# An attention and mixer kernel on one core: tables, first normalizations and transform pieces of the front dealt out over its steps

## The chip, the core and the metric

The kernel runs on one core of a Trainium2 chip. A core has a matrix engine (TensorE, PE in the profile; its weight loads are a row of their own, PEld), a vector engine (DVE), a scalar engine (ACT), a general engine (POOL) and a queue of transfers (SP). Each engine takes its instructions in the order in which they are written for it, and waits at an instruction until what it reads is there and the place it writes is free. Products are accumulated in PSUM, and from there DVE and ACT fetch them; the other tiles lie in SBUF. The metric is the device time of one execution, in microseconds (us): the kernel before took 987.98 in the median of three runs.

## The reference

Three stages follow one another. Inputs are 4 batches, 8 heads, 576 tokens, 64 numbers per head.

```python
# 1. attention in a window of 64 keys
scores = scale * q @ k.T                        # scale = 1/8
scores = where(0 <= query - key < 64, scores, -1e9)
x = softmax(scores) @ v                         # -> [4, 576, 512]
# 2. Fourier mixing, then a channel mixer
u = x + real(fft(fft(x, axis=1), axis=2))
un = (u - mean(u)) / sqrt(var(u) + 1e-6)        # per token
x = u + relu(un @ w_ch1) @ w_ch2                # 512 -> 2048 -> 512
# 3. token mixer, then a second channel mixer
h = relu(x.T @ w_tok1) @ w_tok2                 # 576 -> 256 -> 576
u = x + h.T
out = u + relu(u @ w_ch1b) @ w_ch2b             # 512 -> 1536 -> 512
```

The weights of the mixers come as 64-bit floats.

## The kernel before

**Precision.** Products of stages 2 and 3 are made of two parts of each number: `split` (L125) casts a tile to a rounded 32-bit format on ACT (L127, the `hi` part) and subtracts this from the source on DVE (L130, the `lo` part); three products (hi hi, hi lo, lo hi) stand for one.

**Stage 1** is cut into 36 units, nine for each batch: a tile of 128 queries and four of the eight heads. Unit k goes through scores `s` on PE (L353, L360), their maximum `mx` on DVE (`a_mx`, L369), the exponentials `pb` on ACT (L379), a transposition `pt` on PE (L386) with its copy on ACT (`a_cp`, L389), the product `o` with V on PE (L399), and a division on DVE.

**The transforms** of stage 2 are one per batch. `fold` (L425) adds and subtracts rows of `x` that lie mirrored, and splits the result (tiles `pmt`, `eo`, `xh`; the middle rows in `fold_m`, `xs`). `fft` (from L458) is a generator of 16 chunks: eight of the first transform along the tokens (`zp`, evicted and split as `zt`, L477), two of a small rest (`zx`), and six of the second one along the channels (`bp`, `ap`, tile `t3`), whose results POOL adds to `x`. They multiply by constant tables: `cs` (two tiles of 3 x 320 columns, `load_cs`) and `dd` (4 x 258 columns, `load_dd`), with a row `nyq`.

**The normalization** `prep` (L598) of a group of 384 rows takes their mean and variance on DVE, writes normalized rows `una` on ACT, transposes them on PE (`tpa`, L629) and splits them into `aT`.

**The weights** are converted by `converter` (L148): one piece of 128 x 512 goes through ACT (L162), five DVE instructions (L163 to L165, L178, L179), a multiplication by the exponent on POOL (L181; on DVE once `tailing` is over 10), a cast on ACT (L174) and a subtract on DVE (L184). A call of `conv(1)` takes one of the three parts of such a conversion.

**The channel mixer** runs over six groups of 384 rows and 16 pieces f of the hidden width. `gemm1` (L638) makes twelve matmuls into `zg`; `gemm1_ev` takes the positive part on ACT (L645) and its rest on DVE (L646, `hh`); `gemm2` (L656) makes nine into `acc`, three products later. The first two groups go together through the f, so 32 products use each weight as it is converted; the rest follows in a second pass.

**What sets the order.** All this is written in `front_body` (L863) inside a hand-made schedule: what the Python code calls first stands first in each engine's queue. A loop of 39 steps k issues the stages of units k, k-1 and k-2, up to two chunks of a transform, and then side work as long as a budget `left` lasts: each step adds `CFG["dve"]` = 3.35 less the unit's own work, each piece takes off an estimate. The first table is split at k = 3, the second at 5, `dd` at 7; conversions begin at k = 8; `prep` of group 0 begins at 20 and of group 1 at 30. Behind the loop the rest of the transform of the last batch is written in a tail of chunks n, with a step of the channel mixer (`next(gph)`) at every fourth n, a part of a conversion at odd n, and a part of group 1's `prep` at even ones. After that the mixer goes on alone, one `conv` after each product. DMAs of inputs are asked for in front of the loop and at fixed steps in it, on SP's queue.

## Time and profile before

| | |
|---|---|
| runs | 986.79, 987.98, 988.15 us (median 987.98) |
| the profiled execution | 986.48 us, of which 984.7 are the span of the trace |
| PE, busy | 948.2 us (96%) |
| PE weight loads | 817.7 us (83%) |
| DVE | 521.6 us (53%), 1067 instructions |
| ACT | 288.9 us (29%), 647 instructions |
| POOL | 104.1 us (11%) |
| DMA | 105.47 MB, mean 107 GB/s |

The span is the time from the first to the last instruction in the trace. The page shows these shares in 40 slices of 24.6 us each:

```profile
PE   8998988599999999999999999999999999999998
...
DVE  3777677899999265677675324456321212121121
ACT  4655554333333223232232212223211111111110
POOL 0003032242222001112111000000000000000000
PEclk9789989799999999999999999999999999999999
```

Each digit is a busy share in tenths; PEclk is the clock granted to PE in tenths of its full speed. The loop over the units ends in slice 7, the first two groups of the channel mixer run up to about slice 13. From there the DVE has little to do. A shown share of PE near 90% is not PE at its peak, since the ends of its matmuls are modelled.

### The profile page before, as it was taken

The page shows a single profiled execution, that of the slowest core. Times are in us where ns is not written, and L with a number is a line of the kernel's source. Part 1 is how long each engine was busy: PE and PEld are TensorE (multiplying, and loading weights), DVE is VectorE, ACT ScalarE, POOL GpSimd, SP SyncE. Part 2 cuts the span into 40 slices and gives each one's busy share as a digit, 9 for nine tenths or more (in the row PEclk, how much of TensorE's full clock was granted, in tenths as well). Part 3 has the DMA queues.
Part 4 walks back from the last instruction along what each step waited for, and adds up shares of the span by engine and source line. Part 5 has one row for each costly group of instructions (what it writes and reads, how often), then busy time and mean ns, then how long its engine had stood idle before and what let it go on. Part 6 is the DMA issues. An engine that isn't in the chain of part 4 may idle for free.

```text
span 984.7 us, 14125 instructions
## 1 busy us (share of the span) xinstructions
PE 948.2 (96%) x5576; PEld 817.7 (83%) x5576; DVE 521.6 (53%) x1067; ACT 288.9 (29%) x647; POOL 104.1 (11%) x108
## 2 busy tenths in 40 slices
PE   8998988599999999999999999999999999999998
PEld 5676766588887899999999988878999999999997
DVE  3777677899999265677675324456321212121121
ACT  4655554333333223232232212223211111111110
POOL 0003032242222001112111000000000000000000
PEclk9789989799999999999999999999999999999999
DMA  9843320234353052454543216377110100101010
GB/s 335 283 136 124 115 66 23 91 117 135 118 151 96 14 180 75 145 180 152 180 163 130 80 31 217 109 252 234 29 65 1 56 10 31 35 4 61 1 33 33
DMA packets 56454, 105.47 MB, mean 107 GB/s; under 512 B 5058, under 2 KB 25604, under 8 KB 56004
## 3 DMA queue, kind: packets, MB, share of 16 engines
q1 hardware_dynamic: 55700, 104.24, 32.6%
q8 instruction: 44, 0.72, 0.3%
q10 hardware_dynamic: 688, 0.33, 0.1%
q14 instruction: 22, 0.18, 0.1%
HBM read 79.78 MB, written 24.77 MB: 106 GB/s over the span
## 4 chain that ended last, share of the span: by engine, by line
PE 67%; DVE 13%; issue 1%; ACT 1%; DMA 1%; POOL 0%; DVEq 0%; SPq 0%; ACTq 0%; POOLq 0%
PE zg L638 31%; PE acc L656 31%; PE zt L753 2%; PE zt L728 2%; DVE we L165 2%; DVE wm L179 2%; PE tpa L629 1%; DVE w2s L184 1%; DVE w1s L184 1%; DVE hh L646 1%; DVE rw L178 1%; DVE we L163 1%; DVE we L164 1%; DMA x2r<-x_d 0%; DMA x_d<-o 0%
## 5 line engine op out<-in xcount | busy, mean ns | idle before, releaser
L638 PE MATMUL zg<-aT,w1s 128*128 128x384 f32 x2016 | 388.7, 340 | 3.9 <-DVE hh L646 2.9
L656 PE MATMUL acc<-w2s,hh 128*128 128x512 f32 x1512 | 381.5, 394 | 0.0
L638 PEld LDWEIGHTS zg<-aT,w1s 128*128 128x128 f32 x2016 | 354.9, 189 | 25.9 <-DVE hh L646 13.0
L656 PEld LDWEIGHTS acc<-w2s,hh 128*128 128x128 f32 x1512 | 281.4, 188 | 51.6
L646 DVE SCALAR_TENSOR_TENSOR hh<-zg,hh 128x384 fp32r<-128x384 f32 x168 | 93.3, 556 | 283.6 <-ACT hh L645 283.4
L645 ACT ACTIVATE hh<-zg 128x384 fp32r<-128x384 f32 x168 | 82.4, 491 | 380.5 <-PE zg L638 380.3
L181 POOL TENSOR_TENSOR wm<-wm,we 128x512 f32<-128x512 f32 (+2 forms) x64 | 70.6, 1104 | 346.9 <-DVE wm L179 300.7
L162 ACT ACTIVATE wm<-rw 128x512 f32<-128x512 uint32 (+2 forms) x66 | 41.9, 634 | 78.7 <-DVE w2s L184 40.3
L130 DVE TENSOR_TENSOR aT<-tpa,aT 128x512 fp32r<-128x512 f32 x36 | 24.9, 692 | 41.3 <-ACT aT L127 41.2
L179 DVE SCALAR_TENSOR_TENSOR wm<-rw,wm 128x512 f32<-128x512 int32 (+2 forms) x66 | 43.4, 658 | 5.2
L386 PE MATMUL pt<-ident,pb 128*128 128x128 f32 x144 | 34.0, 333 | 11.1 <-ACT pb L379 10.9
L165 DVE SCALAR_TENSOR_TENSOR we<-rw,we 128x512 uint16<-128x512 uint16 (+2 forms) x66 | 43.5, 659 | 2.0
L360 PE MATMUL s<-kT,qT 64*64 64x128 f32 x576 | 43.3, 294 | 0.0
L360 PEld LDWEIGHTS s<-kT,qT 64*64 64x64 f32 x576 | 34.0, 144 | 10.8 <-issue 10.8
L379 ACT ACTIVATE pb<-s,nb 128x128 f32<-128x128 f32 x144 | 41.2, 369 | 1.3
L386 PEld LDWEIGHTS pt<-ident,pb 128*128 128x128 f32 x144 | 19.1, 149 | 21.7 <-ACT pb L379 13.5
L127 ACT CAST aT<-tpa 128x512 fp32r<-128x512 f32 x36 | 21.0, 586 | 53.2 <-PE tpa L629 53.2
L399 PEld LDWEIGHTS o<-vt,pb 128*64 128x64 f32 x576 | 22.0, 151 | 10.2 <-ACT pb L389 4.5
L399 PE MATMUL o<-vt,pb 128*64 128x65 f32 x576 | 27.3, 243 | 3.2 <-ACT pb L389 3.2
L178 DVE TENSOR_SCALAR rw<-rw 128x512 int32<-128x512 int32 (+2 forms) x66 | 27.6, 418 | 2.0
L163 DVE TENSOR_SCALAR we<-rw 128x512 uint16<-128x512 uint16 (+2 forms) x66 | 28.3, 429 | 0.6 <-DMA rw<-in_moe_w_ch_dram 0.2
L369 DVE TENSOR_REDUCE mx<-s 128x4 f32<-128x512 f32 x36 | 24.5, 682 | 6.3 <-PE s L360 6.3
(128 smaller groups left out, 747.1 us busy)
## 6 DMA issues: line engine op xcount, KB each, us to landing
rw<-in_moe_w_ch_dram SPq DMA_DIRECT2D x56, 512.0 KB, 3.7
vt<-in_vx_dram SPq DMA_DIRECT2D x16, 520.0 KB, 6.7
ur<-u_d SPq DMA_DIRECT2D x28, 256.0 KB, 4.1
wb_d<-wm SPq DMA_DIRECT2D x24, 256.0 KB, 3.0
rf<-wb_d SPq DMA_DIRECT2D x12, 512.0 KB, 4.3
kT<-in_kt_dram SPq DMA_DIRECT2D x3, 1536.0 KB, 10.7
qT<-in_qt_dram SPq DMA_DIRECT2D x8, 512.0 KB, 5.2
x_d<-o SPq DMA_DIRECT2D x16, 256.0 KB, 3.4
```

Source lines behind the costliest of these rows:

```text
L162: held("a", nc.scalar.activation(out=m, in_=low, func=AF.Copy, scale=2.0 ** -52, bias=1.0))
L165: nc.vector.scalar_tensor_tensor(out=e, in0=top, scalar=0x8000, in1=e, op0=ALU.bitwise_and, op1=ALU.bitwise_or)
L179: nc.vector.scalar_tensor_tensor(out=m, in0=high, scalar=2.0 ** -20, in1=m, op0=ALU.mult, op1=ALU.add)
L181: eng.tensor_tensor(out=m, in0=m, in1=e.bitcast(BF16), op=ALU.mult)
L360: nc.tensor.matmul(s4[64 * bl:64 * bl + 64, c, :], lhsT=q_t[b, t // 2][64 * r:64 * r + 64, c, q0:q0 + 64], rhs=kT[b][64 * r:64 * r + 64, c ...
L379: nc.scalar.activation(out=pb[:, 0, c], in_=s4[:, c], func=AF.Exp, bias=nb[:, c:c + 1], scale=scale)
L386: nc.tensor.transpose(pt[:, c, :], pb[:, 0, c, :], ident)
L399: mm = nc.tensor.matmul(o[64 * bl:64 * bl + 64, c, :], lhsT=pb[:, 1, c, 64 * bl:64 * bl + 64], rhs=rhs)
L638: nc.tensor.matmul(zp, lhsT=W[f, 0][:, a, d, :], rhs=res["aT"][:, c, d, :], start=n == 0, stop=n == 11)
L645: nc.scalar.activation(out=h[:, 0], in_=zp, func=AF.Relu)
L646: nc.vector.scalar_tensor_tensor(out=h[:, 1], in0=zp, scalar=0.0, in1=h[:, 0].bitcast(F32), op0=ALU.max, op1=ALU.subtract)
L656: nc.tensor.matmul(res["acc"][c], lhsT=h[:, a, 128 * c:128 * c + 128], rhs=W[f, 1][:, w, :], start=f == 0 and i == 0, stop=f == NF - 1 and ...
```

## The change

It does five things, all in the front. (1) The tables are split in ten pieces, one a step from k = 1 on, and `nyq` in a piece of its own; before, whole at k = 3, 5 and 7. (2) Transform chunks of batch b begin at k = 9b + 13 at the earliest, and in the steps with k % 9 of 2 or 3 one is issued and not two; more of the last transforms comes to stand in the tail. (3) Conversions in the loop begin at k = 11 and not 8. (4) `prep` of group 0 begins at k = 21 and writes its three `una` before the first transposition; its last parts are given a step each from k = 28 on, and those of group 1 one or two a step from k = 31 (`q1`), ten of them inside the loop. (5) Behind the loop a mixer step stands at once, the folds that are left are finished, and the tail has fixed places: mixer steps at six n (`tg`), parts of `prep` at three (`tp`), parts of conversions at eleven (`tc`).

```diff
     def load_cs(g):
...
-        def go():
-            hi = blk([128, 3, KN], F32R, name="cs_hi")
-            lo = blk([128, 3, KN], F32R, name="cs_lo")
-            split(hi, lo, rt, nc.scalar, nc.vector)
-            for j in range(3):
-                csm[divmod(3 * g + j, 2)] = (hi[:, j, :], lo[:, j, :])
-        return go
+        hi = blk([128, 3, KN], F32R, name="cs_hi")
+        lo = blk([128, 3, KN], F32R, name="cs_lo")
+        for j in range(3):
+            csm[divmod(3 * g + j, 2)] = (hi[:, j, :], lo[:, j, :])
+        return [lambda j=j: split(hi[:, j], lo[:, j], rt[:, j], nc.scalar, nc.vector) for j in range(3)]
...
     def load_dd():
...
+        out = [lambda j=j: split(hi[:, j], lo[:, j], rt[:, j], nc.scalar, nc.vector) for j in range(4)]
+        out.append(lambda: nc.vector.tensor_copy(out=nyq, in_=r))
+        return out
...
     def prep(l, src, g, norm, res, keep=True, pt=pm, ts=None):
...
+        ahead = manual[0] and keep
+        if ahead:
+            us = []
+            for c in range(NCH):
+                us.append(unit(c))
+                yield 0.1
         for c in range(NCH):
...
+            a = us[c] if ahead else unit(c)
+            if not ahead:
+                yield 0.1
             tp = pt("tpa").rearrange("p (c n) -> p c n", c=4)
...
     def gphase(l, W, NF, src, dst, norm, extra):
...
-                else:
+                elif not tailing[0]:
                     next(nxt, None)
...
     def front_body():
...
-            later = [load_cs(0), load_cs(1)]
+            later = load_cs(0) + load_cs(1)
...
             def chunk():
                 while cur or ffts:
                     if not cur:
+                        if k < 9 * ffts[0] + 13:
+                            return None
                         cur.append(fft(ffts.pop(0)))
...
-                for _ in range(2):
-                    e = chunk() if k >= 2 else None
+                for _ in range(1 if k % 9 in (2, 3) else 2):
+                    e = chunk() if k >= 13 else None
...
+                if k >= 28 and side0:
+                    t = next(side0[0], None)
...
+                if k == 30:
+                    pre1[0] = prep(0, u_d, 1, True, res[1, 0], ts=x_of(1))
+                for _ in range(2 if k >= NU else 1):
+                    if k >= CFG["q1"] and qcount < 10:
+                        left -= next(pre1[0])
+                        qcount += 1
                 while side and left > 0.0:
...
-                if k in (3, 5):
+                if k >= 1 and later:
                     later.pop(0)()
-                    left -= 1.1
+                    left -= 0.4
                     if k == 3:
-                        later.append(load_dd())
-                if k == 7:
-                    later.pop(0)()
+                        later += load_dd()
...
-                if k == 20:
+                if k == 21:
                     side0.append(prep(0, u_d, 0, True, res[0, 0], ts=x_of(0)))
...
-                while k >= 8 and left > 0.0 and njob[0] < 2 * KA:
+                while k >= 11 and left > 0.0 and njob[0] < 2 * KA:
...
+            next(gph)
+            for t in side:
+                drain(t)
...
             n = 0
             tailing[0] = 1
             while True:
-                if n % 4 == 0:
+                if n in CFG["tg"]:
                     next(gph)
...
-                if n % 2:
+                if n in CFG["tp"]:
+                    next(pre1[0], None)
+                elif n in CFG["tc"]:
                     conv(1)
-                elif n >= 4:
-                    next(pre1[0], None)
...
+ 'q1': 31,
+ 'tg': (2, 4, 6, 9, 11, 14),
+ 'tp': (3, 5, 7),
+ 'tc': (4, 6, 8, 9, 10, 11, 12, 13, 14, 15, 16),
```

In the listings that follow, a row is one kind of instruction (line, operation, out<-in, shape) in the order of its engine. The lines of the changed kernel are 3 lower up to the change in `prep`, and 7 higher behind it.

ACT, at the first table `cs`. Before, from the copy `pb<-pt` of unit 0 on:

```order
L389 COPY pb<-pt 128x512
L371 ACTIVATE nb<-mx 128x4
L379 ACTIVATE pb<-s_178,nb 128x128 x4
L389 COPY pb<-pt 128x512
L371 ACTIVATE nb<-mx 128x4
L379 ACTIVATE pb<-s_205,nb 128x128 x4
L389 COPY pb<-pt 128x512
L371 ACTIVATE nb<-mx 128x4
L379 ACTIVATE pb<-s_245,nb 128x128 x4
L127 CAST cs_hi<-r_cs 128x960
L389 COPY pb<-pt 128x512
```


And now, from the same place:

```order
L386 COPY pb<-pt 128x512
L368 ACTIVATE nb<-mx 128x4
L376 ACTIVATE pb<-s_182,nb 128x128 x4
L127 CAST cs_hi<-r_cs 128x320
L386 COPY pb<-pt 128x512
L368 ACTIVATE nb<-mx 128x4
L376 ACTIVATE pb<-s_211,nb 128x128 x4
L127 CAST cs_hi<-r_cs 128x320
L386 COPY pb<-pt 128x512
```


The cast of the whole table stood behind the exponentials of unit 3. Its first third now stands behind those of unit 1 and ahead of unit 1's copy, and the second third one step later.

DVE, between two neighbouring rows `hh` of the first two groups in the tail. Before:

```order
L646 SCALAR_TENSOR_TENSOR hh<-zg,hh 128x384
L527 TENSOR_TENSOR t_2596<-ap,t_2596 64x257
L528 TENSOR_TENSOR t_2596<-ap,t_2596 64x257
L184 TENSOR_TENSOR w1s<-wm,w1s 128x512
L163 TENSOR_SCALAR we<-rw 128x512
L164 TENSOR_SCALAR we<-we 128x512
L165 SCALAR_TENSOR_TENSOR we<-rw,we 128x512
L178 TENSOR_SCALAR rw<-rw 128x512
L179 SCALAR_TENSOR_TENSOR wm<-rw,wm 128x512
L646 SCALAR_TENSOR_TENSOR hh<-zg,hh 128x384
```


And now, between the rows that answer to them (the end of the stretch is shown):

```order
L163 TENSOR_SCALAR we<-rw 128x512
L164 TENSOR_SCALAR we<-we 128x512
L165 SCALAR_TENSOR_TENSOR we<-rw,we 128x512
L178 TENSOR_SCALAR rw<-rw 128x512
L179 SCALAR_TENSOR_TENSOR wm<-rw,wm 128x512
L184 TENSOR_TENSOR w2s<-wm,w2s 128x512
L163 TENSOR_SCALAR we<-rw 128x512
L164 TENSOR_SCALAR we<-we 128x512
L165 SCALAR_TENSOR_TENSOR we<-rw,we 128x512
L178 TENSOR_SCALAR rw<-rw 128x512
L179 SCALAR_TENSOR_TENSOR wm<-rw,wm 128x512
L653 SCALAR_TENSOR_TENSOR hh<-zg,hh 128x384
```


Before, one conversion (L163 to L179) and one subtract (L184) stand between two hh. Now two conversions stand there.

PE, at the first product of the channel mixer (`zg`), after the loop. Before:

```order
L523 MATMUL ap<-nyq,zx 64x258 x2
L477 MATMUL zp<-cs_hi,xh 128x320
L477 MATMUL zp<-cs_lo,xh 128x320
L477 MATMUL zp<-cs_hi,xh 128x320 x2
L477 MATMUL zp<-cs_lo,xh 128x320
L477 MATMUL zp<-cs_hi,xh 128x320
L477 MATMUL zp<-cs_hi,xs 128x320
L477 MATMUL zp<-cs_lo,xs 128x320
L629 MATMUL tpa<-ident,una 128x128 x4
L638 MATMUL zg<-aT,w1s 128x384 x12
```


And now:

```order
L645 MATMUL zg<-aT,w1s 128x384 x12
L636 MATMUL tpa<-ident,una 128x128 x4
L517 MATMUL ap<-dd_hi,zt 64x258
L517 MATMUL ap<-dd_lo,zt 64x258
L517 MATMUL ap<-dd_hi,zt 64x258 x2
L517 MATMUL ap<-dd_lo,zt 64x258
L517 MATMUL ap<-dd_hi,zt 64x258
L520 MATMUL ap<-nyq,zx 64x258 x2
L474 MATMUL zp<-cs_hi,xh 128x320
L474 MATMUL zp<-cs_lo,xh 128x320
L474 MATMUL zp<-cs_hi,xh 128x320 x2
L645 MATMUL zg<-aT,w1s 128x384 x12
```


Before, a whole chunk pair `zp` of the last transform and the transposition `tpa` stand ahead of the first `zg`. Now `zg` stands first, and `tpa`, the last part of batch 2's transform (`ap`) and half a `zp` stand between it and the second one.

## Rows read from the trace of the kernel before

**Rows 1.** Windows: from:to, length, busy of PE, PEld, DVE, ACT, POOL, clock, DMA share, GB/s.
```profile
25.00:35.00 10.00, 10.00 (x85) 7.76 (x86) 7.05 (x17) 6.35 (x19) 0.00 (x0) 0.50 0.75 251
162.40:235.00 72.60, 58.25 (x324) 49.42 (x324) 63.63 (x124) 27.07 (x55) 25.50 (x27) 0.88 0.33 106
235.00:319.70 84.70, 82.63 (x393) 68.94 (x392) 80.46 (x149) 30.05 (x57) 22.09 (x19) 1.00 0.41 121
```

**Rows 2.** DVE timeline, units: start, us, line, op, tiles, shapes, count, [idle before, releaser].
```profile
14.21 0.69 DVE L369 TENSOR_REDUCE mx<-s 128x4 f32<-128x512 f32 x1 [1.73 <-PE s L360]
...
21.40 1.16 DVE L130 TENSOR_TENSOR cs_lo<-r_cs,cs_hi 128x960 fp32r<-128x960 f32 x1 [3.30 <-ACT cs_hi L127]
22.47 0.68 DVE L369 TENSOR_REDUCE mx<-s 128x4 f32<-128x512 f32 x1
...
23.81 0.68 DVE L369 TENSOR_REDUCE mx<-s 128x4 f32<-128x512 f32 x1
...
36.50 1.23 DVE L130 TENSOR_TENSOR dd_lo<-r_dd,dd_hi 128x1032 fp32r<-128x1032 f32 x1 [2.65 <-ACT dd_hi L127]
...
55.74 0.68 DVE L369 TENSOR_REDUCE mx<-s 128x4 f32<-128x512 f32 x1
```

**Rows 3.** ACT timeline around the first table.
```profile
13.68 1.15 ACT L379 ACTIVATE pb<-s,nb 128x128 f32<-128x128 f32 x4
...
20.37 0.99 ACT L127 CAST cs_hi<-r_cs 128x960 fp32r<-128x960 f32 x1 [0.67 <-DMA r_cs<-in_c_cs_dram]
...
23.43 1.14 ACT L379 ACTIVATE pb<-s,nb 128x128 f32<-128x128 f32 x4
```

**Rows 4.** PE timeline, the first matmul of the scores of two neighbouring units.
```profile
28.97 0.63 PE L353 MATMUL s<-cap,idb 128*128 128x512 bf16 x1
...
33.41 0.63 PE L353 MATMUL s<-cap,idb 128*128 128x512 bf16 x1
```

**Rows 5.** Groups by shape, 10 to 205 us: busy us, mean ns, idle before, releaser.
```profile
L425 DVE TENSOR_TENSOR pmt<-xp 128x512 f32<-128x512 f32 x5 | 4.7, 941 | 0.0
...
L130 DVE TENSOR_TENSOR zt<-zp,zt 128x320 fp32r<-128x320 f32 x16 | 7.9, 492 | 15.1 <-ACT zt L127 15.1
...
L127 ACT CAST zt<-zp 128x320 fp32r<-128x320 f32 x16 | 7.0, 437 | 1.7 <-PE zp L477 1.7
...
L425 DVE TENSOR_TENSOR pmt<-x 128x512 f32<-128x512 f32 x3 | 2.1, 688 | 0.1
```

**Rows 6.** DVE timeline from the last unit's maximum to the eighth hh.
```profile
162.40 0.66 DVE L369 TENSOR_REDUCE mx<-s 128x4 f32<-128x512 f32 x1
...
186.86 0.56 DVE L646 SCALAR_TENSOR_TENSOR hh<-zg,hh 128x384 fp32r<-128x384 f32 x1 [0.23 <-ACT hh L645]
...
216.05 0.55 DVE L646 SCALAR_TENSOR_TENSOR hh<-zg,hh 128x384 fp32r<-128x384 f32 x1
...
230.57 0.55 DVE L646 SCALAR_TENSOR_TENSOR hh<-zg,hh 128x384 fp32r<-128x384 f32 x1
231.03 1.40 DVE L184 TENSOR_TENSOR w2s<-wm,w2s 128x512 fp32r<-128x512 f32 x1
232.36 0.41 DVE L163 TENSOR_SCALAR we<-rw 128x512 uint16<-128x512 uint16 x1
...
235.00 0.55 DVE L646 SCALAR_TENSOR_TENSOR hh<-zg,hh 128x384 fp32r<-128x384 f32 x1
```

**Rows 7.** PE timeline after the last unit.
```profile
174.74 0.63 PE L477 MATMUL zp<-cs_hi,xh 128*128 128x320 f32 x1 [4.48 <-ACT xh L127]
...
182.24 4.06 PE L638 MATMUL zg<-aT,w1s 128*128 128x384 f32 x12 [0.68 <-ACT aT L127]
...
188.48 2.28 PE L638 MATMUL zg<-aT,w1s 128*128 128x384 f32 x12
```

**Rows 8.** DVE timeline behind the last conversion of the first two groups.
```profile
324.81 0.56 DVE L646 SCALAR_TENSOR_TENSOR hh<-zg,hh 128x384 fp32r<-128x384 f32 x1 [3.69 <-ACT hh L645]
...
328.94 0.56 DVE L646 SCALAR_TENSOR_TENSOR hh<-zg,hh 128x384 fp32r<-128x384 f32 x1 [3.58 <-ACT hh L645]
```

More of the change, by code (lines that the diff above doesn't have):

```diff
@@ L287, in load_dd @@
             ldq.dma_start(out=rt[:, 2 * m:2 * m + 2, :], in_=c_dd[m])
-        def go():
-            nc.vector.tensor_copy(out=nyq, in_=r)
-            hi = blk([128, 4, LN], F32R, name="dd_hi")
-            lo = blk([128, 4, LN], F32R, name="dd_lo")
-            split(hi, lo, rt, nc.scalar, nc.vector)
-            for m in range(2):
-                for cs in range(2):
-                    ddm[m, cs] = (hi[:, 2 * m + cs, :], lo[:, 2 * m + cs, :])
-        return go
+        hi = blk([128, 4, LN], F32R, name="dd_hi")
+        lo = blk([128, 4, LN], F32R, name="dd_lo")
+        for m in range(2):
+            for cs in range(2):
+                ddm[m, cs] = (hi[:, 2 * m + cs, :], lo[:, 2 * m + cs, :])
+        out = [lambda j=j: split(hi[:, j], lo[:, j], rt[:, j], nc.scalar, nc.vector) for j in range(4)]
+        out.append(lambda: nc.vector.tensor_copy(out=nyq, in_=r))
+        return out
     kT = {}
@@ L618, in prep, with unit @@
         res["aT"] = aT
-        for c in range(NCH):
-            u = ts[c]
-            if norm:
-                a = un([128, DM], F32, name="una")
-                nc.scalar.activation(out=a, in_=u, func=AF.Identity, scale=y[:, c:c + 1], bias=nm[:, c:c + 1])
-            else:
-                a = u
-            yield 0.1
+        def unit(c):
+            if not norm:
+                return ts[c]
+            a = un([128, DM], F32, name="una")
+            nc.scalar.activation(out=a, in_=ts[c], func=AF.Identity, scale=y[:, c:c + 1], bias=nm[:, c:c + 1])
+            return a
+        ahead = manual[0] and keep
[4 more added lines that the diff above has]
+                yield 0.1
+        for c in range(NCH):
+            a = us[c] if ahead else unit(c)
+            if not ahead:
+                yield 0.1
             tp = pt("tpa").rearrange("p (c n) -> p c n", c=4)
@@ L825, in gphase @@
                             ncount[0] += 1
-                else:
+                elif not tailing[0]:
                     next(nxt, None)
@@ L919, in front_body @@
                         side.append(fold_m(b))
+                if k >= 28 and side0:
+                    t = next(side0[0], None)
+                    if t is None:
+                        side0.pop(0)
+                    else:
+                        left -= t
+                if k == 30:
[4 more added lines that the diff above has]
+                        qcount += 1
                 while side and left > 0.0:
@@ L954, in front_body @@
                         load_q(b, 2)
-                if k == 20:
+                if k == 21:
                     side0.append(prep(0, u_d, 0, True, res[0, 0], ts=x_of(0)))
-                if k == 30:
-                    pre1[0] = prep(0, u_d, 1, True, res[1, 0], ts=x_of(1))
-                while side0 and left > 0.0 and (pcount < 7 or k >= 28):
+                while side0 and left > 0.0 and pcount < 7:
                     t = next(side0[0], None)
@@ L967, in front_body @@
                         break
-                while k >= 30 and left > 0.0 and qcount < 7:
-                    left -= next(pre1[0])
-                    qcount += 1
-                while k >= 8 and left > 0.0 and njob[0] < 2 * KA:
+                while k >= 11 and left > 0.0 and njob[0] < 2 * KA:
                     conv(1)
@@ L976, in front_body @@
                     side0.pop(0)
+            while qcount < 10:
+                next(pre1[0])
+                qcount += 1
+            next(gph)
+            for t in side:
+                drain(t)
+            assert (B - 1, 2) in fst
+            if not ffts:
+                ffts.append(B - 1)
+            k = 99
             n = 0
```

1 line of the change is left out of this document (added).

## The prediction

> **What bounds the kernel now.** I read the windows by stage first, then the VectorE (DVE) and ScalarE (ACT) timelines of the front, the groups by shape, and last the rows where TensorE (PE) idles. The stretch after the front is the place to begin. From 235.00 to 319.70 us the DVE is busy 80.46 of 84.70 us [rows 1]. PE is shown busy 82.63 us there, but that is a modelled share and not its limit: products follow one another in 4.43 us (hh at 230.57 and 235.00) while one conversion of a weight piece stands between them on the DVE [rows 6], and in 4.13 us (324.81 to 328.94) once the conversions are over and the DVE idles 3.58 us before each hh [rows 8]. So the DVE sets the pace up to the last conversion, and PE from there to the end. The stage before it, from the last unit's maximum at 162.40 to the eighth hh at 235.00, has the DVE busy 63.63 of 72.60 us [rows 1].
>
> In the loop over the units the DVE also sets the pace: every step waits for ACT's first half of a split (zt, 16 of them, 15.1 us idle before them, 0.95 us each) [rows 5]. Only at the start is the pace another's: ACT's cast of the first table waits for its transfer until 20.37 us, and the DVE idles 3.30 us behind it [rows 2, 3]. So a change is worth what it alters in the order of DVE rows, and in its waits.
>
> **The start, steps 0 to 11.** Before, the first table is split in step 3. Now its first third is asked for in step 1, and on ACT it stands ahead of the copy of unit 1's transposed weights. Its data come from the same place in SP's queue, so it can't run before 20.37 [rows 3]; ACT is through with unit 1's exponentials at 13.68 + 1.15 = 14.83 and stands still 5.5 us, and the DVE's subtract waits with it, with unit 2's maximum behind it, and PE's products with V of unit 1 behind ACT's copy. The cast of a third costs 0.44 and its subtract 0.49 (the same 128x320 shape as zt) [rows 5]: unit 2's maximum starts near 20.37 + 0.44 + 0.49 = 21.3. In steps 2 to 4 each maximum is followed by exponentials and then by a piece: from a maximum at 22.47 to the end of its exponentials at 23.43 + 1.14 = 24.57 are 2.1 us [rows 2, 3], and a cast and subtract of 0.93 behind them, less the pipeline overlap of about 0.2, give 2.8 us a step. Unit 5's maximum comes at 21.3 + 3 x 2.8 = 29.7, where it was 23.81 [rows 2]: 5.9 us late.
>
> Much of that is bought back, since whole tables no longer stop later steps. From 23.81 to 55.74 were 31.9 us [rows 2]. Out go the second table's subtract (1.16), the transform table's subtract with its wait (1.23 + 2.65 = 3.9) [rows 2], and the better part of two conversions: the DVE part up to the multiply is 2.64 us (from 232.36 to 235.00) [rows 6], of which only the first three instructions (some 1.5) remain, 2 x 2.64 - 1.5 = 3.8. In come six pieces of 0.49, 2.9 us, and in two steps that have nothing else to do while ACT finishes, 0.95 of wait each, 1.9. That makes 31.9 - 1.2 - 3.9 - 3.8 + 2.9 + 1.9 = 27.8, and unit 12's maximum at 57.5 instead of 55.74, +1.8.
>
> PE's clock adds to it. From 25 to 35 us the granted clock is 0.50, the lower of its two levels, and a step of PE (scores to scores, 28.97 to 33.41) takes 4.44 us there [rows 1, 4]. With ACT standing still, PE runs dry for more than 4 us, so I expect the half clock again, and a step of 2.8 us becomes one of 4.4. Five of the next steps (2, 3, 4, 7, 8) are shorter than 4.4: at most 5 x 1.6 = 8 us; none, if the clock holds. Work for the DVE in the longer steps hides most of it. I take 0.7, and **+2.5 us** in all, between -1 (the pieces fill only idle time) and +9.8.
>
> **The middle, steps 12 to 34.** The rows balance: in come two halves and one head of the deferred conversions (2 x 1.1 + 1.5) and one more split of a transposed chunk (0.6), 4.3 us; out go one fold with its split (3.2), one subtract of a weight (0.6) and one zx (0.4), 4.2. What goes with them is one wait for ACT (0.95 [rows 5]). And by dealing the third part of a transform over two steps, its POOL sums move away from the folds: a fold's 128x512 addition takes 941 ns in the mean where POOL is at work on the same rows, and 688 where it isn't [rows 5], so some five such rows save 0.25 each, 1.3. **-2.2 us**, between -6 (every clock spell gone too) and +3 (the longest steps stay).
>
> **After the last unit.** Here lies the largest term. Up to the eighth hh the new order gives the DVE more to do. Two conversions more: at the fourth hh both orders have finished eight, then the old one does one per product and the new one two between some of them, so that 14 instead of 12 are done at the eighth. With the one that was not finished in the loop that is 2 x 2.64 for the heads, and three subtracts of 0.6, 7.1 us. Two multiplications by the exponent that POOL did now stand on the DVE, 0.6 each, 1.2. The fold and split of the last transform's first half have slipped out of the loop: two of 0.65 (pmt [rows 5]), and by their smaller sizes two of 0.35, one of 0.2 and one of 0.6, 2.8. One zx more (0.4), one transposed chunk less (0.6). The sum is +10.9.
>
> Against it stand waits that go. Before, PE finds nothing for 4.48 us at 170.26 to 174.74 [rows 7], and the first hh comes 186.86 - 162.40 = 24.5 us after the last maximum [rows 6] behind DVE rows that take 16.7 together (the rows of the order between the two, each at the mean of its shape), 7.8 us of waits and stretched rows. The first product is now issued as soon as the loop ends, its normalized rows being ready, and the DVE has a fold to do in the gap; I let 2.2 of the 7.8 go. The two multiplications taken from POOL also free two subtracts that stand beside one: 1.40 with it [rows 6] against 0.6, so 1.5 saved. 10.9 - 2.2 - 1.5 = **+7.2** at the eighth hh. In detail: the first hh 2 us earlier than now, the fourth about 5 us earlier (48.5 after the last maximum, now 216.05 - 162.40 = 53.7 [rows 6]), the eighth 7 later (80, now 72.6).
>
> What the two early conversions give back is little: the last two products of the stretch run at PE's 4.13 us instead of the DVE's 4.43 [rows 6, 8], -0.6. PE can't make up the rest, as it is then the bound itself. So **+6.6 us**, between -5 (the lead at the fourth hh is kept) and +10.
>
> **The sum.** 2.5 - 2.2 + 6.6 = +6.9 on the profiled execution's 986.48 us (span 984.7 and 1.8 around it), 993.4. The median of the runs, 987.98, is 1.5 above that execution: 994.9. After 320 us the instructions stand in the same order, so nothing is gained or lost there.
>
> **Rivals.**
> *The filled gap decides (faster).* PE's first product at 182.24 takes 4.06 us after the idle spells, the second 2.28 [rows 7]; the new order has two products and a transform half to put there. If from the fourth hh on PE and not the DVE sets the pace, its lead of 5.2 us there is kept: 2.5 - 2.2 - 5.2, 986.48 - 4.9 + 1.5 = 983.1. For it too: the loop has idle time left that an even dealing could fill, 15.1 us in front of zt alone [rows 5], of which my middle counts next to nothing. Against it: 80.46 of 84.70 us of the DVE after the front [rows 1], work that no order takes away.
> The Trainium skill's page "Perfetto Trace Analysis" (Optimizing Scalar/DVE Operations) speaks for this side: where these engines aren't saturated but leave bubbles on others, breaking instructions up may let work finish sooner. By that rule the pieces would help, since the DVE has 3.30 us of idleness at the first table; the row shows that this idleness is a transfer's, which no piece shortens.
> The page "TensorE: Matmul & The Clock Gate" of the Trainium skill (Part 1) says that the slow clock is the default and activity lifts it; the pair 4.06 and 2.28 agrees, and by it alone the fuller tail would win some 2 us on one product.
> *The terms cancel.* The middle gains its 6 and the start costs its 2.5 while the tail loses 3: 987.5, no change.
> *The slow clock stays through the start.* If PE runs at half clock in steps 2 to 8 the start costs 9.8 instead of 2.5: 1002.2. For it: ten microseconds at 0.50 in the kernel before, without so long a wait in front of them [rows 1]. Against it: steps of over 4 us cover most.
> *The even dealing changes nothing.* Seven more subtracts and casts for the same tables, DVE rows in the middle equal to 0.1 us: then only the tail counts, 994.6, inside the forecast.
>
> **Chances.** The forecast (990 to 999) 0.44; the slow clock (999 to 1005) 0.11; cancelled (within 986 to 990) 0.15; the kept lead, faster, 0.30, since it needs only that the waits in the loop and the gap close by more than I count. A measurement of this kernel tells about 0.2%, 2 us, from no change, so slower 0.55, same 0.15, faster 0.30. The range 981 to 1001 leaves out the better part of the faster case (some 0.10) and the worse of the slow clock. The forecast alone stands at 990 to 999.
>
> **What would show it.** In the new profile: ACT's first cast at 20.4 with some 5.5 us idle before it, and unit 2's maximum at 21.3; unit 12's at 57 to 59; the last unit's maximum within 3 us of 162.4; the first hh 22 us behind it, the eighth near 80; the last conversion with eight, not six, of the 32 products of the first two groups still to come; the slices at 12 to 20 us with PE idle. I am wrong if unit 2's maximum is at 14, if the loop ends before 157, or if the eighth hh comes 73 us or less after the last maximum.

## The result and the profile after

The changed kernel took 1000.06 us in the median of four runs (997.39 to 1000.74), beside 988.07 of the kernel before in the same comparison: a ratio of 1.0117, with a 95% interval from 1.0095 to 1.0139. It is 12 us slower; the prediction said 994.9, slower, in a range from 981 to 1001. The profiled execution took 1000.28 us, with a span of 998.5, 13.8 more than before.

Three lines of the page, in 40 slices of 25 us, show where to look: the busy tenths of PE and DVE, and PE's granted clock.

```profile
PE   7998989687999999999999999999999999999998
...
DVE  2677777899999257477676233456421212112121
...
PEclk8679889598999999999999999999999999999999
```

From slice 13 on the two kernels look alike; in the first twelve PEclk falls lower and in other places than before. So I divide the 13.8 us at three marks on the DVE: unit 12's maximum (55.74 before [rows 2]), the last unit's (162.40) and the eighth hh (235.00) [rows 6]. These are the timeline rows of the changed kernel that answer to them: unit 2's, unit 5's, unit 12's and the last unit's maximum, and the first, fourth and eighth hh.

```profile
21.45 0.68 DVE L366 TENSOR_REDUCE mx<-s 128x4 f32<-128x512 f32 x1
...
31.20 0.68 DVE L366 TENSOR_REDUCE mx<-s 128x4 f32<-128x512 f32 x1
...
61.01 0.68 DVE L366 TENSOR_REDUCE mx<-s 128x4 f32<-128x512 f32 x1
...
167.34 0.66 DVE L366 TENSOR_REDUCE mx<-s 128x4 f32<-128x512 f32 x1
...
188.96 0.56 DVE L653 SCALAR_TENSOR_TENSOR hh<-zg,hh 128x384 fp32r<-128x384 f32 x1 [0.26 <-ACT hh L652]
...
215.62 0.55 DVE L653 SCALAR_TENSOR_TENSOR hh<-zg,hh 128x384 fp32r<-128x384 f32 x1
...
248.18 0.56 DVE L653 SCALAR_TENSOR_TENSOR hh<-zg,hh 128x384 fp32r<-128x384 f32 x1
```

| stretch | before | after | difference | predicted |
|---|---|---|---|---|
| to unit 12's maximum | 55.74 | 61.01 | +5.3 | +2.5 |
| from there to the last unit's | 106.66 | 106.33 | -0.3 | -2.2 |
| from there to the eighth hh | 72.60 | 80.84 | +8.2 | +7.2 |
| from there to the end of the span | 749.7 | 750.3 | +0.6 | -0.6 |

Differences of about one us in this table are within what one order varies by from one execution to the next: up to the last unit the kernel before has the same order in a later run (the lead in conversions spent, below), and there unit 12's maximum stands at 54.42 and the last unit's at 162.04.

The start. ACT's first cast stands and waits for its table, and the DVE stands behind it. First ACT's row, then the DVE's, with the idle time and what ended it in brackets:

```profile
20.55 0.46 ACT L127 CAST cs_hi<-r_cs 128x320 fp32r<-128x320 f32 x1 [5.31 <-DMA r_cs<-in_c_cs_dram]
20.92 0.58 ACT L386 COPY pb<-pt 128x512 f32<-128x512 f32 x1
```

```profile
21.04 0.49 DVE L130 TENSOR_TENSOR cs_lo<-r_cs,cs_hi 128x320 fp32r<-128x320 f32 x1 [8.16 <-ACT cs_hi L127]
21.45 0.68 DVE L366 TENSOR_REDUCE mx<-s 128x4 f32<-128x512 f32 x1
...
23.93 0.49 DVE L130 TENSOR_TENSOR cs_lo<-r_cs,cs_hi 128x320 fp32r<-128x320 f32 x1 [1.05 <-ACT cs_hi L127]
24.34 0.68 DVE L366 TENSOR_REDUCE mx<-s 128x4 f32<-128x512 f32 x1
```

Two different waits are seen here. The first, 8.16 us, ends with a transfer; the second, 1.05, is a piece's own: the subtract follows its cast at once, and the next unit's maximum stands behind it. It comes back in the next step (1.05) and, where PE runs at its lower clock (0.50 from 27 to 31 us), as 2.15 in the one behind: that step takes 3.97 us, from 27.23 to unit 5's maximum at 31.20, and the two ahead of it 2.89 each.

The tail. These are the windows from the last unit's maximum to the eighth hh and from there to the end of the last conversion:

```profile
167.34:248.18 80.84, 62.51 (x323) 53.11 (x322) 73.90 (x146) 29.18 (x60) 25.55 (x27) 0.81 0.34 103
248.18:324.50 76.32, 74.42 (x362) 64.08 (x361) 71.44 (x133) 26.56 (x51) 19.79 (x17) 1.00 0.41 126
```

The DVE is busy 73.90 us in the first where it was 63.63 [rows 1], 10.3 more; its idle time is 6.9 instead of 9.0, 2.0 less.

### The profile page after: what moved, and what is told of

It reads as the page before. It is cut to its first block, busy times and chain, and to the rows that moved or that the text cites. A ratio compares the mean times of both kernels' runs of the same rounds, so it can differ in the third digit from the quotient of the medians.

```text
span 998.5 us, 14134 instructions
## 1 busy us (share of the span) xinstructions
PE 959.0 (96%) x5576; PEld 830.3 (83%) x5576; DVE 520.6 (52%) x1076; ACT 290.2 (29%) x654; POOL 100.4 (10%) x106
## 4 chain that ended last, share of the span: by engine, by line
PE 66%; DVE 11%; DMA 2%; issue 1%; ACT 1%; POOL 0%; DVEq 0%; SPq 0%; ACTq 0%
PE acc L663 30%; PE zg L645 30%; PE zt L760 2%; PE zt L735 2%; DVE we L165 2%; DVE wm L179 1%; DMA rw<-in_moe_w_ch_dram 1%; PE tpa L636 1%; DVE we L163 1%; DVE w2s L184 1%; DVE rw L178 1%; DVE hh L653 1%; DVE w1s L184 1%; DVE we L164 1%; DMA x_d<-o 0%
## 5 line engine op out<-in xcount | busy, mean ns | idle before, releaser
L181 POOL TENSOR_TENSOR wm<-wm,we 128x512 f32<-128x512 f32 (+3 forms) x62 | 69.0, 1112 | 370.5 <-DVE wm L179 324.9
L357 PEld LDWEIGHTS s<-kT,qT 64*64 64x64 f32 x576 | 37.2, 155 | 12.5 <-issue 11.9
L357 PE MATMUL s<-kT,qT 64*64 64x128 f32 x576 | 47.2, 312 | 0.0
L179 DVE SCALAR_TENSOR_TENSOR wm<-rw,wm 128x512 f32<-128x512 int32 (+2 forms) x66 | 42.9, 650 | 5.2
L165 DVE SCALAR_TENSOR_TENSOR we<-rw,we 128x512 uint16<-128x512 uint16 (+2 forms) x66 | 43.5, 660 | 2.1
L163 DVE TENSOR_SCALAR we<-rw 128x512 uint16<-128x512 uint16 (+2 forms) x66 | 31.3, 474 | 2.0 <-DMA rw<-in_moe_w_ch_dram 1.6
L178 DVE TENSOR_SCALAR rw<-rw 128x512 int32<-128x512 int32 (+2 forms) x66 | 27.2, 413 | 2.0
L386 ACT COPY pb<-pt 128x512 f32<-128x512 f32 x36 | 21.1, 586 | 24.1 <-PE pt L383 23.4
```

The source lines that it names most:

```text
L163: held("c", nc.vector.tensor_scalar(out=e, in0=top, scalar1=0x7FF0, scalar2=None, op0=ALU.bitwise_and))
L165: nc.vector.scalar_tensor_tensor(out=e, in0=top, scalar=0x8000, in1=e, op0=ALU.bitwise_and, op1=ALU.bitwise_or)
L179: nc.vector.scalar_tensor_tensor(out=m, in0=high, scalar=2.0 ** -20, in1=m, op0=ALU.mult, op1=ALU.add)
L181: eng.tensor_tensor(out=m, in0=m, in1=e.bitcast(BF16), op=ALU.mult)
L357: nc.tensor.matmul(s4[64 * bl:64 * bl + 64, c, :], lhsT=q_t[b, t // 2][64 * r:64 * r + 64, c, q0:q0 + 64], rhs=kT[b][64 * r:64 * r + 64, c ...
```

## The experiments

Twelve kernels ran, each timed in alternation with the kernel before; they fall into four comparisons: the first four sections, the next three, the three after these, and the last one. Medians of the kernel before in them: 987.45, 987.82, 988.12 and 987.51; the changed kernel was timed in one of its own (988.07). Where numbers of different comparisons stand side by side, their ratios to the kernel before count. Marks in us are those of one profiled execution of each kernel.

### Whole tables again

```diff
...
-                if k >= 1 and later:
-                    later.pop(0)()
-                    left -= 0.4
+                if k in (3, 5):
+                    later.pop(0)()
+                    left -= 1.1
...
+                if k == 7:
+                    later.pop(0)()
```

> The changed kernel with its tables split whole again, at k = 3, 5 and 7; all else as changed. Theory 1 (the first third's wait for its transfer at k = 1 delays the units, and the delay lasts): unit 2's maximum back near 14, unit 12's near 56 where the changed kernel has 61.0, the last unit's near 162.5, and 995 us in all, 5 less than the changed kernel's 1000. Theory 2 (the start is made good later, since the steps behind it wait less): the last unit's maximum stays near 167 and the time near 1000. Theory 3 (pieces are better once they are there): the start gains 7, the whole tables cost 3 again, 996.

Measured: 990.67 us, ratio 1.0036 [1.0021, 1.0052]. The dealing from k = 1 on carries two thirds of the whole loss (1.0117). Unit 12's and the last unit's maxima, on the DVE:

```profile
51.71 0.68 DVE L367 TENSOR_REDUCE mx<-s 128x4 f32<-128x512 f32 x1
...
158.07 0.66 DVE L367 TENSOR_REDUCE mx<-s 128x4 f32<-128x512 f32 x1
```

Unit 12 comes 9.3 us earlier than in the changed kernel, and 4.0 earlier than in the kernel before; the last unit is 9.3 earlier as well. So the delay lasts to the end of the loop (theory 1), but it is twice what theory 1 gave. The rest of the change gains 4 us in the first twelve units, where one conversion stands now instead of two: the step from unit 8's to unit 9's maximum takes 1.34 us (37.10 to 38.44), where it took 4.18 (37.65 to 41.83). The kernel before with later conversions alone, below, is as early at unit 12 (51.31).

### The first table's transfer earlier

```diff
             load_k(0, (576, KW))
+            later = load_cs(0)
             load_v(0, 1)
...
-            later = load_cs(0) + load_cs(1)
+            later += load_cs(1)
```

> The changed kernel with the transfer of the first table asked for earlier, ahead of V of units 2 and 3; the pieces stay one a step from k = 1. Theory 1 (the wait for the transfer is the cost, not the dealing): ACT's first cast near 15 instead of 20.55, unit 2's maximum near 15.5 instead of 21.45, unit 12's near 56, 995 us. Theory 2 (a cast and a subtract in each short step are the cost, since every maximum waits for ACT): the first cast at 15, but unit 12's maximum still at 60 and the time 999. Theory 3 (half clock): like theory 1 if the clock of 25 to 40 us comes back to 1, like theory 2 if it stays at 0.5.

Measured: 990.02 us, ratio 1.0031 [1.0019, 1.0043]; theory 1's cause, again with a larger size. The clock of 25 to 45 us is 1.00 here, so theory 3 isn't told from theory 1 by this run; the next one does that. The cast starts at 14.95 without a wait, and unit 12's maximum comes at 51.27, with all ten pieces dealt out:

```profile
15.86 0.69 DVE L366 TENSOR_REDUCE mx<-s 128x4 f32<-128x512 f32 x1
...
51.27 0.69 DVE L366 TENSOR_REDUCE mx<-s 128x4 f32<-128x512 f32 x1
...
157.21 0.66 DVE L366 TENSOR_REDUCE mx<-s 128x4 f32<-128x512 f32 x1
```

With its data there, the dealt start is about as long as that with whole tables (51.27 beside 51.71). This does not show that dealing itself is free, since the whole first table still waited for its transfer (the DVE idle 3.07 us): in the kernel before, below, the earlier transfer alone brings unit 12 forward by 2.1 us. By that the pieces would cost 0.3 to 1.6 us in this place, an estimate (with unit 12 at 54.42 or 55.74 in the two traces of the order before); whole tables with the earlier transfer were not run in the changed kernel. What cost most was that the first piece stood in the queue ahead of its data.

### PE filled during the wait

```diff
                     a_s(k)
+                if k == 3:
+                    wp = pa("warm")
+                    for i in range(20):
+                        nc.tensor.matmul(wp, lhsT=idb, rhs=cap, start=True, stop=True)
```

> The changed kernel with twenty products of constants (bf16, 128 x 512, result never read) on PE at k = 3, ahead of the product of unit 1 with V, where PE is idle 4.53 us. Theory 1 (the wait itself is the cost): the clock may rise, but unit 12's maximum stays at 61 within 1 and the time at 1000. Theory 3 (the lower clock that follows the idle PE is half of the cost): the windows of 25 to 40 us at 1.0 instead of 0.5 to 0.6, unit 12's maximum at 58, the time 997.

Measured: 996.79 us, ratio 1.0100 [1.0081, 1.0120]. By the times alone this can't be told from the changed kernel's 1.0117; by the trace it can. The wait stays (the first cast at 20.84, the DVE idle 8.78 in front of its subtract), the products fill PE for 4.49 us, and the clock of the steps behind is another. The windows of this kernel, and then the same of the changed kernel:

```profile
14.00:25.00 11.00, 9.67 (x96) 5.51 (x92) 2.55 (x7) 4.12 (x13) 0.00 (x0) 1.00 0.90 349
25.00:45.00 20.00, 18.18 (x247) 12.49 (x242) 14.10 (x40) 14.58 (x46) 0.00 (x0) 1.00 0.74 264
```

```profile
14.00:25.00 11.00, 6.33 (x76) 4.49 (x73) 2.84 (x8) 4.44 (x14) 0.00 (x0) 0.74 0.88 344
25.00:45.00 20.00, 20.00 (x183) 15.24 (x179) 11.70 (x32) 10.91 (x36) 0.00 (x0) 0.55 0.50 161
```

The clock's column reads 1.00 instead of 0.55, and PE issues 247 matmuls in those 20 us instead of 183. Unit 12's maximum:

```profile
57.15 0.68 DVE L366 TENSOR_REDUCE mx<-s 128x4 f32<-128x512 f32 x1
```

It comes 3.9 us earlier than the 61.01 of the changed kernel, the last unit's 4.1 earlier (163.20). So theory 3 holds for the loop: of the 9.74 us between 51.27 and 61.01, 5.88 are the wait and 3.86 go with the lower clock behind it.

The Trainium skill's page "TensorE: Matmul & The Clock Gate" (Part 1) says that the slow clock is the default and that activity of the array lifts it; this trace agrees, 1.00 behind the filled stretch and 0.55 behind the empty one.

### The tail placed as before

```diff
-                elif not tailing[0]:
+                else:
                     next(nxt, None)
...
-            next(gph)
             for t in side:
                 drain(t)
...
-                if n in CFG["tg"]:
+                if n % 4 == 0:
                     next(gph)
...
-                if n in CFG["tp"]:
-                    next(pre1[0], None)
-                elif n in CFG["tc"]:
-                    conv(1)
+                if n % 2:
+                    conv(1)
+                elif n >= 4:
+                    next(pre1[0], None)
```

> The changed kernel with the tail's placing as before: a mixer step at every fourth n, parts of conversions at odd n, no mixer step ahead of the folds; the loop stays as changed. Theory 1 (my term for the tail, 8.2 us in the two traces at the eighth hh): the eighth hh 73 to 75 us after the last maximum instead of 80.8, 992 to 993 us. Theory 2 (the tail costs because chunks slipped into it from the loop, wherever it places them): the eighth hh still at 80, 1000 us.

Measured: 992.70 us, ratio 1.0059 [1.0038, 1.0081]; theory 1. The last maximum and the eighth hh:

```profile
163.74 0.66 DVE L366 TENSOR_REDUCE mx<-s 128x4 f32<-128x512 f32 x1
...
238.42 0.55 DVE L653 SCALAR_TENSOR_TENSOR hh<-zg,hh 128x384 fp32r<-128x384 f32 x1
```

That is 74.68 us for the way, 6.2 less than the 80.84 of the changed kernel; 2.1 stay; the chunks that slipped into the tail would account for them, which no run tests by itself. This trace is also a second look at the start: up to the last unit the instructions are those of the changed kernel, yet unit 12's maximum came at 57.51, with the clock of 25 to 45 us at 0.89. The same order was 3.5 us faster in this execution than in that with 0.55, so what goes with the clock varies from one execution to another.

### Fewer conversion parts in the tail

```diff
- 'tc': (4, 6, 8, 9, 10, 11, 12, 13, 14, 15, 16),
+ 'tc': (4, 8, 11, 13, 16),
```

On top of the earlier transfer.

> The changed kernel with the earlier transfer of the first table (990.0 us without more), and in its tail five parts of conversions at fixed places instead of eleven, so that two conversions less stand ahead of the eighth hh; the place of every chunk and mixer step stays. Theory 1 (DVE rows are the limit up to the eighth hh, and the lead in conversions isn't given back later): the eighth hh about 73 us after the last maximum instead of 81.0, 983 us. Theory 2 (the three waits of acc for the rows t of the transform are the limit, which hold PSUM places): the eighth hh at 79 or more, 988 to 990 us.

Measured: 984.29 us, ratio 0.9965 [0.9953, 0.9978]; theory 1. From the last maximum to the eighth hh, here and then in the kernel with the earlier transfer and eleven parts:

```profile
157.19:230.55 73.36, 59.13 (x322) 50.88 (x320) 65.20 (x132) 27.18 (x56) 24.76 (x27) 0.86 0.30 97
157.21:238.20 80.99, 62.35 (x325) 52.69 (x323) 74.02 (x146) 29.36 (x60) 25.56 (x27) 0.83 0.32 103
```

73.36 us, 7.6 less than with the eleven parts. The DVE's busy time fell by 8.8 from 74.02 and its idle time rose by 1.2. The changed kernel's PE shows three waits of acc for the transform's PSUM places in that stretch (2.65, 0.93 and 2.77 us), two of them for rows t on the DVE. Here, with two conversions less in front of these rows and the chunks in the same places, none of the three is left: they followed from the DVE's queue and were no limit of their own.

```profile
238.47 0.94 PE L663 MATMUL acc<-w2s,hh 128*128 128x512 f32 x3 [2.65 <-DVE t L525]
240.33 1.01 PE L663 MATMUL acc<-w2s,hh 128*128 128x512 f32 x3 [0.93 <-ACT t L511]
244.11 1.62 PE L663 MATMUL acc<-w2s,hh 128*128 128x512 f32 x3 [2.77 <-DVE t L525]
```

### Both costs taken away

The edits are those of the earlier transfer and of the old tail.

> The changed kernel with the earlier transfer and the tail placed as before. Theory 1 (the two costs add): unit 12's maximum at 51, the eighth hh 74.7 after the last maximum, 990.0 - 6.2 = 984 us, 3 to 4 below the kernel before. Theory 2 (a loop that ends earlier leaves more to the tail): the eighth hh at 78 and 987 us.

Measured: 984.69 us, ratio 0.9976 [0.9967, 0.9985]; theory 1. The eighth hh stands 74.67 us behind the last maximum (232.29 and 157.62). By the profile and by the ratios the two costs add.

### The lead in conversions spent

```diff
-                conv(CFG["convt"] if tailing[0] else 1)
+                conv(CFG["convt"] if tailing[0] or (nprod[0] > 8 and nprod[0] % 3 == 0) else 1)
```

`nprod` counts the products. The same edit was made in the changed kernel with the earlier transfer, and in the kernel before.

> The changed kernel with the earlier transfer, and from the ninth product on one part of a conversion less at every third product, since the tail has made a lead in conversions. Theory 1 (a product takes 4.43 us only because a whole conversion stands in each): the steps from hh to hh go to 4.15 up to the 24th, 16 x 0.28 = 4.5 us less, 985.5 us; the lead is worth that much if it is spent. Theory 2 (PE needs the 4.43 for other reasons): the steps stay at 4.4 and the time at 990.

> The kernel before with the same thinning from its ninth product on; nothing else is changed. Its conversions then end at the 28th product instead of the 26th, still in time for the weights. Theory 1: steps of 4.15 instead of 4.43 up to the 26th, 17 x 0.28 less 2 x 0.3 for the two products that lose their free ride, 983 to 984 us. Theory 2: 987.5, no change.

Measured: the first 985.81 us, ratio 0.9980 [0.9969, 0.9991], some 5 us less by the ratios than without the edit (1.0031), as theory 1 had it. The second 988.63 us, ratio 1.0015 [1.0004, 1.0026]: my expectation of a gain was wrong. There the eighteenth hh comes 4.4 us earlier (275.08, where before it stood at 279.44), but the last conversions come later, and PE waits for their weights. PE's rows of the kernel before with the edit:

```profile
317.50 0.62 PE L639 MATMUL zg<-aT,w1s 128*128 128x384 f32 x2 [1.63 <-ACT w1s L175]
320.67 3.57 PE L639 MATMUL zg<-aT,w1s 128*128 128x384 f32 x10 [2.55 <-DVE w1s L185]
```

The 29th product is the first that needs the last of the sixteen weight pairs. Its hh comes at 324.79, as before (324.81), and the next three lose 1.3 us, the 32nd standing at 342.92 (341.64 before): behind the two waits the granted clock is 0.52 from 320.6 to 327 us, 1.00 in the same window of the kernel before. Without a lead the DVE is busy up to there in any order, and a product that is given less of a conversion only hands it on. A lead is worth something only where it can be spent.

### The subtract one step behind its cast

```diff
...
-                    later.pop(0)()
+                    if subs:
+                        subs.pop(0)()
+                    if later:
+                        cast, sub = later.pop(0)
+                        cast()
+                        subs.append(sub)
```

On top of the earlier transfer and the five parts of conversions. `cast` and `sub` are the two halves of `split`, given apart.

> The kernel with the earlier transfer and five conversion parts in the tail (984.3 us), in which DVE subtracts each dealt piece one step after ACT has cast it. Theory 1 (in the short steps the next maximum waits behind a subtract that waits for ACT, 1.05 us in each of four steps): those waits gone, steps of 2.4 instead of 2.9 us, unit 12's maximum 2 to 4 us earlier (47 to 49), 981 us. Theory 2 (ACT or PE is the limit in these steps as well): the steps stay at 2.8, unit 12's at 51, 984 us.

Measured: 980.79 us, ratio 0.9938 [0.9922, 0.9953]; theory 1. This kernel beats the kernel before by 0.6%, and the changed one by 1.8%. The DVE of this kernel in steps 2 and 3, and unit 12's maximum:

```profile
15.13 0.69 DVE L370 TENSOR_REDUCE mx<-s 128x4 f32<-128x512 f32 x1 [1.74 <-PE s L361]
...
16.49 0.48 DVE L272 TENSOR_TENSOR cs_lo<-r_cs,cs_hi 128x320 fp32r<-128x320 f32 x1
17.57 0.69 DVE L370 TENSOR_REDUCE mx<-s 128x4 f32<-128x512 f32 x1 [0.59 <-PE s L361]
...
47.63 0.68 DVE L370 TENSOR_REDUCE mx<-s 128x4 f32<-128x512 f32 x1
```

The subtract has no wait, a step takes 2.44 us instead of 2.89, and the DVE now waits 0.59 for PE's scores.

The Trainium skill's page "Perfetto Trace Analysis" (Optimizing Scalar/DVE Operations) holds that breaking instructions up may let work finish sooner where ACT and DVE aren't saturated but leave other engines idle. Here the pieces with an earlier transfer gave nothing over whole tables (51.27 beside 51.71); 3.6 us were won (47.63 beside 51.23 in the kernel that this one is built on) once the second half of a piece no longer waited for the first.

### Later conversions in the kernel before

The edit is `k >= 11` for `k >= 8` in the loop of conversions.

> The kernel before, with conversions in the loop beginning at k = 11 instead of 8, and nothing else changed. Theory 1 (the later conversions are what puts unit 12's maximum at 51.7 where the tables are whole, 4.0 us before the kernel before; they come later in the loop, since the budget hands them to later steps): unit 12's at 52, the last unit's at 161 to 162.4, 987 us. Theory 2 (the gain lasts, later steps have idle DVE time to cover them): unit 12's at 52, the last unit's at 158.5, 983.5 us.

Measured: 992.81 us, ratio 1.0050 [1.0033, 1.0066], worse than both theories. Unit 12's maximum comes early, as expected, but the next one is 7 us away, and the last 1.6 later than before:

```profile
51.31 0.68 DVE L369 TENSOR_REDUCE mx<-s 128x4 f32<-128x512 f32 x1
...
58.35 0.68 DVE L369 TENSOR_REDUCE mx<-s 128x4 f32<-128x512 f32 x1
...
163.97 0.68 DVE L369 TENSOR_REDUCE mx<-s 128x4 f32<-128x512 f32 x1
...
240.19 0.55 DVE L646 SCALAR_TENSOR_TENSOR hh<-zg,hh 128x384 fp32r<-128x384 f32 x1
```

The budget hands the deferred conversions out at once, two parts of them (L178 and L179, then L163 to L165) in the step behind unit 12. From unit 12 to the last unit are 112.7 us, 6.0 more than in the kernel before, where the changed kernel, with the same later start, has 106.3: its other moves in the loop made up for the deferred conversions there. The way to the eighth hh is 76.2 us instead of 72.6. So the later start by itself is no gain. Three conversions instead of four had gone through L179 when the loop ended, so some of the tail's growth is a part that slipped into it; the rest was not traced.

### The earlier transfer in the kernel before

> The kernel before, with the transfer of the first table asked for ahead of V of units 2 and 3. Theory 1 (its whole table, too, is cast only when the transfer is there, DVE idle 3.30 us): unit 4's maximum at 20 instead of 22.47, unit 12's at 53, 985 us. Theory 2 (V or Q of the units behind come late instead): unit 4's at 22 or later, 987.5 us or more.

Measured: 985.57 us, ratio 0.9981 [0.9970, 0.9991]; theory 1 in the time, though unit 4's maximum came only at 21.93 and unit 12's at 53.66. The kernel before had a small part of the same cost.

### The transforms dealt as before

```diff
-                for _ in range(1 if k % 9 in (2, 3) else 2):
-                    e = chunk() if k >= 13 else None
+                for _ in range(2):
+                    e = chunk() if k >= 2 else None
...
-                        if k < 9 * ffts[0] + 13:
-                            return None
```

On top of the kernel with late subtracts.

> The kernel of the run before with late subtracts (980.8 us), its transforms dealt as in the kernel before: two chunks in every step and no earliest step; tables, normalizations and tail stay as they are there. Theory 1 (the spacing is worth about as much as my term for the middle, since fewer sums of POOL fall beside folds): the last unit's maximum 1 to 3 us later than 153.9, the time 982 to 984 us. Theory 2 (the spacing only moves work from the loop to the tail): the last unit's maximum 2 to 4 us later, the way from there to the eighth hh as much shorter than its 73.3, the time 980 to 981.5 us. Theory 3 (the spacing costs, like the other moves into the tail): 978 us.

Measured: 990.87 us, ratio 1.0034 [1.0022, 1.0046], some 9.5 us by the ratios slower than with the spacing (0.9938): more than any theory gave. The last maximum and the eighth hh, here and then in the kernel with late subtracts:

```profile
156.28 0.66 DVE L370 TENSOR_REDUCE mx<-s 128x4 f32<-128x512 f32 x1
...
231.87 0.56 DVE L657 SCALAR_TENSOR_TENSOR hh<-zg,hh 128x384 fp32r<-128x384 f32 x1
```

```profile
153.87 0.66 DVE L370 TENSOR_REDUCE mx<-s 128x4 f32<-128x512 f32 x1
...
227.19 0.56 DVE L657 SCALAR_TENSOR_TENSOR hh<-zg,hh 128x384 fp32r<-128x384 f32 x1
```

The loop takes 2.4 us more and the way to the eighth hh 2.3 more; another 2.7 come by the 32nd product, since one conversion less had been done at the eighth (a part of it fell behind in the fixed places of the tail, which weren't fitted to this dealing). That makes 7.4 in the traces up to there; the two profiled executions differ by 5.8 in all (988.85, the fastest of its kernel, and 983.01, the slowest of its own). The spacing is a gain, in the loop 2.4 us in this pair of traces, and little of it by POOL: the first addition of the five folds takes 855 ns here and 859 there, the second 860 and 772, 0.4 us for the five. Which of its two rules gains stays open, and what the spacing alone is worth in a tail that is fitted to either dealing.

## Why the prediction was right, and where it was off

The direction was right, for the reason given: the order of DVE rows, and one wait that the first piece put in front of them. The size was less well met. 1000.06 lies above the forecast of 990 to 999 and in the band of the slow clock (999 to 1005), which had a chance of 0.11; it is 0.9 us inside the range. Two signs missed: unit 12's maximum came at 61.01 and not at 57 to 59, and the last unit's 4.9 us from 162.4 and not within 3. That the range held is in part luck, since the clock decided several us. Step by step:

- The first cast (20.4 predicted, 20.55 measured), ACT's idle time (5.5; 5.31), unit 2's maximum (21.3; 21.45) and two of the three short steps (2.8 us; 2.89) came as worked out. The third took 3.97, so unit 5 came at 31.20 and not at 29.7. What the later conversions give back to the first twelve units was about right (3.8; 4.4 where nothing else was changed).
- The start as a whole was mis-sized, +5.3 instead of +2.5, and the term that failed is the clock: "I take 0.7". Without it the wait and the dealing give 57.15 - 55.74 = +1.4, where the prediction had +1.8; the clock added 3.9. I had counted on longer steps to cover it, but from 25 to 45 us the clock's mean was 0.55. The rival of the slow clock named the right mechanism, and its bound of 8 us held; it was neither absent nor full. In the execution with 0.89 the same order stood at 57.51, +1.8: there the term would have been too large, not too small.
- The middle was -0.3 instead of -2.2, and both of the gains that it counted on failed. Here is the stretch between the two marks, before and after, and the two first additions of a fold in it that take longest, in each kernel:

```profile
55.74:162.40 106.66, 95.98 (x1059) 74.24 (x1055) 79.47 (x202) 58.83 (x174) 20.05 (x23) 0.95 0.27 91
61.01:167.34 106.33, 98.68 (x1045) 78.77 (x1044) 78.20 (x201) 60.45 (x176) 20.04 (x24) 0.89 0.31 99
```

```profile
85.15 1.11 DVE L425 TENSOR_TENSOR pmt<-xp 128x512 f32<-128x512 f32 x1
...
127.22 1.12 DVE L425 TENSOR_TENSOR pmt<-xp 128x512 f32<-128x512 f32 x1
```

```profile
90.47 1.12 DVE L422 TENSOR_TENSOR pmt<-xp 128x512 f32<-128x512 f32 x1
...
131.96 1.12 DVE L422 TENSOR_TENSOR pmt<-xp 128x512 f32<-128x512 f32 x1
```

  POOL's sums did not move away from the folds here: two folds stand beside them in both kernels (the sums begin at 84.98 and 127.05 before, at 90.30 and 131.79 now). The mean of the five rows of the front fell from 941 [rows 5] to 859 ns only because of the fold at 170.08, behind the last unit, whose addition took 1.11 us; the two that stand there now take 0.69 each. And the wait for ACT in front of zt did not go: twelve such rows stand in the stretch in both kernels, with 12.3 us of waits before and 13.3 after. The DVE's busy time fell by 1.3 us, and its idle time rose by 0.9.
- The tail was the largest net term, as predicted, and near in size: +8.2 instead of +7.2 at the eighth hh, with the first hh 21.6 and the fourth 48.3 us behind the last maximum, 22 and 48.5 foretold, and two conversions more done at the eighth. Four traces with this tail give 80.54, 80.99, 80.70 and 80.84 us. Their granted clock differs little over the stretch (0.85, 0.83, 0.81 and 0.81), so they don't tell the DVE from PE as its limit; the run with five parts does, where 8.8 us less of DVE work took 7.6 off. With this the rival of the kept lead falls: the lead of 5.4 us at the fourth hh was gone at the eighth.
- Taken away one at a time, the wait at the start with its clock was nevertheless worth more than the tail's placing: 8.5 us by the ratios (1.0117 and 1.0031) beside 5.7 (1.0117 and 1.0059). The table hides this, because the later conversions give 4 us back in the same stretch.
- The early conversions gave nothing back: at the 32nd hh the difference was 13.1 (354.73 and 341.64), as at the eighth 13.2, where I had -0.6. They could have given 5 us, if the products behind them had been thinned out to spend the lead.

The sum of the steps was 993.4 for the profiled execution, which took 1000.28. Of the 6.9 us that lack, 2.8 are in the start, 1.9 in the middle, 1.0 in the tail and 1.2 behind it.

## What to carry to other kernels

In a queue that is served in order, a small piece is as late as its data: before a table is dealt out from an early step on, read when its transfer lands, and ask for it earlier or start later. Put the two halves of a piece that run on two engines into different steps, or each piece adds the first engine's latency to the second. Work done ahead on the bounding engine is only moved, unless something behind it is thinned out to use the lead.

## What was not expected of the hardware

An idle stretch of PE of 4.53 us went with half the clock for most of the 20 us that followed (0.55 in the mean), though PE had work in all of them; twenty unread products in that stretch kept it at 1.00. In the kernel before with thinned conversions, waits of 1.63 and 2.55 us close to each other went with 0.52 in the 6.4 us behind them. The same instructions in another execution had 0.89 from 25 to 45 us and were 3.5 us faster at unit 12, so a few us between two executions of one order go with the clock.
